# Hash attention with an MLP on one core: how queries without a matching key get their value, by a product or by an addition

## The chip, the cores and the metric

One NeuronCore of a Trainium2 chip runs the program. Five engines work in order, each on its own queue, and wait for each other by semaphores: TensorE (PE, matmul; its weight loads are listed as PEld), VectorE (DVE), ScalarE (ACT), GpSimd (POOL) and SyncE (SP, which only issues DMAs). PE writes its results into PSUM, from where DVE and ACT bring them to SBUF. The metric is the device time of one execution in microseconds (us).

## The reference

Queries, keys and values are `[4, 8, 768, 64]` (batch, head, token, width). Six random projections give each query and key a bucket of 6 bits; a query sees only keys of its own bucket.

```python
q_bits = einsum('bhsd,dk->bhsk', q, proj) > 0          # k the same
mask = q_bucket[:, :, :, None] == k_bucket[:, :, None, :]
scores = where(mask, scale * q @ k.T, -1e9)
attn = softmax(scores)                                  # per row
x = (attn @ v), heads side by side                      # [4, 768, 512]
xn = (x - mean) / sqrt(var + 1e-6) * g
out = x + relu(xn @ w1) @ w2                            # 512 -> 2048 -> 512
```

A row without any key of its bucket has only scores of -1e9. After the maximum is taken away they are all equal, so such a query gets the mean of all 768 values of its head. Both kernels compute this without a branch: every key gets an extra weight of `EPS_KEY = 2**-100` in every row. Beside a key that matches this is nothing; where none matches it is all there is, and the quotient is the mean.

## The kernel before

The bits are written as rows 64 to 69 under the transposed queries and keys (`slots`), scaled so that a score with different bits becomes hugely negative; one matmul of 70 rows then gives score and mask at once. The work is cut into 12 chunks of 256 queries (`b`, `t`: batch, third of the tokens). A chunk has four pairs of heads `j`, and each pair three units: PE forms four score tiles (L383, tile `sc`), ACT takes the exponential (L389, `ex`), and PE multiplies by the values (L415), eight products into the PSUM tile `av`. `vaug` holds the values in bf16 with a 65th column of ones, so the sum of weights comes out in column 64. After the third unit DVE takes the reciprocal of that column (L425) and multiplies (L426) into `x`.

The extra weight comes in at the first unit of a pair, by an opener (L406): a product of the constant matrix `epsk` (all `EPS_KEY`) with the values, broadcast over both query tiles. It carries `start=True`, all later products add to it. Its right side is either `vsum`, the sum of the six value blocks of a head, which POOL forms with five additions for half of the heads (`value_sums`, L336 and L339, 128x256 each), or, where that sum is not there in time, the six blocks of `vaug` themselves, in six products. The latter is so in five pairs of batch 0; all other 43 pairs have one opener.

The first 24 units, those of the chunks 0 and 1 with the score tiles of the next unit always formed one step ahead, are written out by hand (`first_two`): a list `seq` gives the units in order, and `also` names what goes between them: transposes of heads (`head`), hash products (`hash_pair`), loads and preparations for the next batch. From then on `interleave` lays each chunk's units out and puts fillers between them by their declared costs: the norm of the chunk before, its eight `up` blocks (L488, hidden layer; tile `hp`, evacuated to `hbuf` in turn by DVE at L129 and ACT at L133), the eight `down` parts of the chunk before that (L505, tile `o`; DVE adds them to `x` at L510, then SP stores), and the parts of `plan` that prepare the next batch: L and W load, N narrows to bf16 (POOL, L239), B and K transpose blocks (DVE, L244), T builds operands by DMA, H hashes, V casts values and sums them (POOL, L330 and L336 to L339), Q takes sums of squares (ACT, L191) for a safety test at the end. The norm gives `xn` (DVE, L450 to L452), `xnT` by a transposing DMA, and `rs` on POOL (L466, L467). After the last chunk come its norm, the downs left over, its ups and its downs. The order of instructions on an engine is that of these lists, but a scheduler may move neighbours.

PSUM: the score tiles have two buffers of two banks, `av` has two, and a third pool, `ps_mm`, has two that all other products share in turn (`hp`, `o`, hash, transposes). A tile of `ps_mm` can start only when DVE or ACT has emptied the buffer that it is given.

In batch 0 `CMAP` changes the order of the key blocks, and heads are transposed by PE instead of by DMA.

Of the kernel before, what the change touches and what calls it, by code (L numbers as in the profile page):

```python
# [9 lines left out]
F32 = mybir.dt.float32  # L10
BF16 = mybir.dt.bfloat16
# [17 lines left out]
def kernel(  # L29
# [11 lines left out]
    nc = tc.nc  # L41
# [57 lines left out]
    ]  # L99
    vsum = [  # L100
        consts.tile([P, H, D1], BF16, name=f"vsum{i}", tag=f"vsum{i}") for i in range(2)
    ]
    for i in range(2):
        nc.gpsimd.memset(vaug[i][:, :, :, D:D1], 1.0)
        nc.gpsimd.memset(vsum[i][:, :, D:D1], float(NC))

# [66 lines left out]
    class Prep:  # L173
# [13 lines left out]
        def squares(self, half, a, j):  # L187

            junk = work.tile([P, 2 * NC * D], BF16, tag="junk", bufs=1, name="junk")
            col = (2 * self.b + half) * 2 + j  # L190
            nc.scalar.activation(  # L191
                junk,
                self.tiles[half]["qk"[a]][:, 2 * j : 2 * j + 2].rearrange("p h c d -> p (h c d)"),
                AF.Square,
                accum_out=sq[:, a, col : col + 1],
            )
# [135 lines left out]
        def value_sums(self, half):  # L332
            hs = slice(half * H // 2, (half + 1) * H // 2)
            vn = self.va[:, hs, :, 0:D]
            acc = work.tile([P, H // 2, D], F32, tag="vacc", bufs=1, name="vacc")
            nc.gpsimd.tensor_add(acc, vn[:, :, 0, :], vn[:, :, 1, :])  # L336
            for c in range(2, NC):
                dst = self.vs[:, hs, 0:D] if c == NC - 1 else acc
                nc.gpsimd.tensor_add(dst, acc, vn[:, :, c, :])  # L339

        def part(self, kind, half):
# [7 lines left out]
            if kind in "BK":  # L349
                return [  # L350
                    (0, lambda a=a, j=j: self.blocks(half, a, j))
                    for a in range(kind == "K", 2) for j in range(2)
                ]
            if kind == "L":
                return [(0, lambda: self.load(half))]
# [9 lines left out]
    def att_units(b, t, x):  # L365
# [4 lines left out]
        for j in range(NP):  # L370
# [7 lines left out]
            for g, grp in enumerate(groups):  # L378
# [17 lines left out]
                def values(grp=grp, g=g, state=state, j=j, ha=ha):  # L396
                    if g == 0:
                        av = ps_av.tile([P, 2, TT, D1], F32, tag="av", name="av")
                        state["av"] = av
                        opens = (  # L400
                            [va[:, ha : ha + 2, c, :] for c in range(NC)]
                            if b == 0 and (t, j) in ((0, 0), (0, 2), (0, 3), (1, 2), (1, 3))
                            else [vs[:, ha : ha + 2, :]]
                        )
                        for i, o in enumerate(opens):
                            nc.tensor.matmul(  # L406
                                av,
                                epsk,
                                o.unsqueeze(2).to_broadcast([P, 2, TT, D1]),
                                start=(i == 0), stop=False, skip_group_check=True,  # L410
                            )
                    av = state["av"]
                    for i, (h, kj) in enumerate(grp):
                        for qi in range(TT):
# [3 lines left out]
                                va[:, h, CMAP[b][kj], :],  # L418
                                start=False,
                                stop=(g == 2 and i == 3),  # L420
                                skip_group_check=True,
                            )
                    if g == 2:
                        rc = work.tile([P, 2, TT], F32, tag="rc", name="rc")
                        nc.vector.reciprocal(rc, av[:, :, :, D])  # L425
                        nc.vector.tensor_tensor(  # L426
                            x[:, :, ha * D : (ha + 2) * D].rearrange(
                                "p t (h d) -> p h t d", h=2
                            ),
                            av[:, :, :, 0:D],  # L430
                            rc.unsqueeze(3).to_broadcast([P, 2, TT, D]),
                            op=AOP.mult,
                        )
# [179 lines left out]
    def first_two():  # L613
# [8 lines left out]
        def keep_awake(n):  # L622
            tp = ps_mm.tile([P, P], F32, tag="mm", name="wakep")
            for _ in range(n):
# [11 lines left out]
        load_w1()  # L636
        prep.value_sums(0)
        groups = [(0, 0), (0, 1), (1, 0), (1, 1), (2, 0), (3, 0), (2, 1), (3, 1)]
# [3 lines left out]
            0: [lambda: head(2), lambda: prep.values(1)],  # L642
            1: [lambda: head(3), lambda: nxt.load(0)],
            3: [lambda: prep.hash_pair(1, 0)],
# [4 lines left out]
            8: [  # L649
                lambda: prep.hash_pair(2, 1), lambda: nxt.load(1), lambda: nxt.load_v(0),  # L650
            ],
# [7 lines left out]
            15: [  # L659
                lambda: nxt.blocks(0, 0, 1), lambda: prep.value_sums(1),  # L660
            ],
# [16 lines left out]
    plan = {  # L678
        2: "K10 H10 N11 B11 V10 W11 | T11 H11 Q00 L20 V11 W20",
        3: "N20 B20 Q01 | T20 H20 L21",  # L680
        4: "V20 W21 Q10 L30 B21 N21 | T21 H21",
        5: "V21 W30 Q11 L31",
        6: "V30 W31 N30 B30 Q20 | T30 H30",
        7: "V31 Q21 B31 N31 | T31 H31",
        8: "Q30 Q31",
# [20 lines left out]
    for n in range(2, len(chunks)):  # L706
# [5 lines left out]
        fillers += mixed(early, tail[:4]) + ([(600, xtrans)] if n == 2 else [])  # L712
        fillers += mixed(late, tail[4:]) + ups
        tail = downs
        if n == NT * (B - 1):
# [197 lines left out]
```

## Time and profile before

| | |
|---|---|
| median of three runs | 327.76 us (326.68 to 327.8) |
| the profiled execution | 326.76 us, span of the profile 324.9 us |
| PE, busy | 306.4 us, 94% |
| weight loads (PEld) | 226.1 us, 70% |
| ACT | 217.3 us, 67% |
| DVE | 163.0 us, 50% |
| POOL | 90.5 us, 28% |
| granted TensorE clock, mean | 0.994 |

The page gives for each engine its busy time, then the span in 40 slices of 8.1 us, where each digit is the busy share in tenths. A group of instructions is one line: source line, engine, operation, output<-inputs, shapes, count; then busy time in us and mean duration of one in ns; then the idle time of the engine just before them and what ended it. Since matmuls overlap, the mean duration of one is longer than the distance from one to the next. The timeline lists instructions in order of time as start, length, engine, line, operation; a row can merge several. The chain of waits goes back from the last instruction to what released it, step by step.

### The profile page before, as it was taken

Reading aid. Unit: us, or ns where it says so; the run is one execution under the profiler, and the core shown is the slowest. Engines: PE = TensorE matmul, PEld = TensorE weight load, DVE = VectorE, ACT = ScalarE, POOL = GpSimd, SP = SyncE. Lnnn points to the kernel's source line nnn. Section 1 sums busy time; section 2 is a strip of 40 time slices with the busy share of each in tenths; the row PEclk is TensorE's granted clock in tenths of the full one; section 3 lists DMA queues with packets and bytes.
Section 4 is the critical chain, followed back from the end, with each engine's and each line's share of the span. In section 5 each row is a group of like instructions: output and inputs, shape, how many; then the busy total and the mean of one; then the engine's idle time right before and its main releaser. Section 6 shows DMA issues by size and latency. Waiting matters only on the chain.

```text
span 324.9 us, 7860 instructions
## 1 busy us (share of the span) xinstructions
PE 306.4 (94%) x3314; PEld 226.1 (70%) x3314; DVE 163.0 (50%) x321; ACT 217.3 (67%) x272; POOL 90.5 (28%) x117
## 2 busy tenths in 40 slices
PE   7958989999989999989999999999999999999992
PEld 5635568768758768759769769658679678687650
DVE  2668967653744654514654753532533623435320
ACT  5647689745766867876966966998657577574110
POOL 4777664662114060236090030200200100201100
PEclk9999999999999999999999999999999999999997
DMA  7999995986197398497255362020120210200301
GB/s 251 357 209 300 209 328 113 227 231 188 33 235 193 103 247 163 112 281 197 48 115 91 61 122 48 12 61 29 32 67 2 48 52 2 65 34 2 98 7 69
DMA packets 64874, 40.94 MB, mean 126 GB/s; under 512 B 47184, under 2 KB 59728, under 8 KB 64832
## 3 DMA queue, kind: packets, MB, share of 16 engines
q1 hardware_dynamic: 60368, 31.85, 39.2%
q0 software_dynamic: 4096, 8.13, 10.6%
q8 instruction: 28, 0.46, 0.6%
q10 hardware_dynamic: 368, 0.39, 0.4%
q14 instruction: 14, 0.11, 0.1%
HBM read 27.98 MB, written 6.88 MB: 107 GB/s over the span
## 4 chain that ended last, share of the span: by engine, by line
PE 73%; DMA 7%; ACT 6%; POOL 5%; DVE 4%; issue 4%; SPq 0%; ACTq 0%; POOLq 0%
PE hp L488 23%; PE o L505 20%; PE sc L383 14%; PE av L415 9%; DMA slots<-nat 4%; ACT junk L191 3%; ACT ex L389 2%; PE hash L275 2%; PE hash L306 2%; DVE slots L326 2%; DMA vnat<-in_v_dram 2%; POOL vaug L330 1%; PE av L406 1%; DMA qnat<-in_q_dram 1%; POOL vacc L339 1%
## 5 line engine op out<-in xcount | busy, mean ns | idle before, releaser
L389 ACT ACTIVATE ex<-sc,expb 128x1024 bf16<-128x1024 f32 x144 | 159.5, 1113 | 67.1 <-PE sc L383 66.9
L488 PE MATMUL hp<-xnT,w_sb 128*128 128x256 bf16 x768 | 98.6, 272 | 0.4 <-ACT hbuf L133 0.3
L505 PE MATMUL o<-w_sb,hbuf 128*128 128x512 bf16 x384 | 96.2, 379 | 0.0
L383 PE MATMUL sc<-slots 70*128 70x256 bf16 x576 | 87.3, 272 | 2.3 <-DVE slots L326 2.1
L488 PEld LDWEIGHTS <-w_sb 128*128 128x128 bf16 x768 | 72.0, 97 | 9.6 <-issue 0.8
L415 PEld LDWEIGHTS <-ex 128*128 128x128 bf16 x1152 | 53.1, 98 | 24.1 <-ACT ex L389 9.2
L415 PE MATMUL av<-vaug,ex 128*128 128x65 bf16 x1152 | 59.3, 194 | 3.8 <-ACT ex L389 3.7
L383 PEld LDWEIGHTS <-slots 70*128 70x128 bf16 x576 | 51.1, 97 | 16.9 <-DVE slots L326 2.6
L129 DVE TENSOR_SCALAR hbuf<-hp 128x512 bf16<-128x512 f32 x45 | 31.1, 691 | 58.4 <-PE hp L488 58.4
L505 PEld LDWEIGHTS <-hbuf 128*128 128x128 bf16 x384 | 35.2, 97 | 27.8
L466 POOL TENSOR_SCALAR rs<-mv 128x2 f32<-128x2 f32 x12 | 5.3, 442 | 168.0 <-DVE mv L451 168.0
L133 ACT ACTIVATE hbuf<-hp 128x512 bf16<-128x512 f32 x51 | 30.4, 596 | 20.9 <-PE hp L488 20.3
L510 DVE SCALAR_TENSOR_TENSOR x<-o,rs,x 128x512 f32<-128x512 f32 x24 | 17.8, 742 | 45.9 <-PE o L505 45.5
L426 DVE TENSOR_TENSOR x<-av,rc 128x256 f32<-128x256 f32 x48 | 20.3, 424 | 1.6
L452 DVE SCALAR_TENSOR_TENSOR xn<-x,mv,gbc 128x512 bf16<-128x512 f32 x24 | 19.5, 834 | 0.4 <-DVE mv L451 0.2
L425 DVE RECIPROCAL rc<-av 128x4 f32<-128x4 f32 x48 | 8.4, 176 | 18.2 <-PE av L415 18.2
L339 POOL TENSOR_TENSOR vacc<-vacc,vaug 128x256 f32<-128x256 f32 x24 | 16.9, 702 | 1.3
L450 DVE BATCH_NORM_STATS2 stats<-x 128x6 f32<-128x512 f32 x24 | 15.3, 677 | 0.2
L330 POOL CAST vaug<-vnat 128x1536 bf16<-128x1536 f32 x8 | 12.5, 1563 | 8.0 <-PE av L415 5.5
L239 POOL CAST nat<-qnat 128x1536 bf16<-128x1536 f32 x6 | 8.8, 1470 | 18.7 <-DMA qnat<-in_q_dram 13.3
L406 PE MATMUL av<-vsum,epsk 128*128 128x260 bf16 x43 | 11.9, 277 | 2.0 <-POOL vsum L339 2.0
L191 ACT ACTIVATE junk<-knat 128x768 bf16<-128x768 f32 x16 | 13.4, 840 | 0.2
(70 smaller groups left out, 195.0 us busy)
## 6 DMA issues: line engine op xcount, KB each, us to landing
out_dram<-x SPq DMA_DIRECT2D x24, 256.0 KB
vnat<-in_v_dram SPq DMA_DIRECT2D x7, 768.0 KB
qnat<-in_q_dram SPq DMA_DIRECT2D x11, 384.0 KB
knat<-in_k_dram SPq DMA_DIRECT2D x11, 384.0 KB
w_sb<-in_moe_w_ch_dram POOLq DMA_DIRECT2D x4, 1024.0 KB, 12.8
slots<-slots SPq DMA_DIRECT2D x6, 384.0 KB
qnat<-in_q_dram POOLq DMA_DIRECT2D x2, 768.0 KB, 11.9
knat<-in_k_dram POOLq DMA_DIRECT2D x2, 768.0 KB, 13.4
```

The costliest lines, as they stand in the source:

```text
L129: nc.vector.tensor_scalar_max(dst, src, 0.0)
L133: nc.scalar.activation(dst, src, AF.Relu if relu else AF.Copy)
L191: nc.scalar.activation(junk, self.tiles[half]["qk"[a]][:, 2 * j : 2 * j + 2].rearrange("p h c d -> p (h c d)"), AF.Square, accum_out=sq[:, ...
L339: nc.gpsimd.tensor_add(dst, acc, vn[:, :, c, :])
L383: nc.tensor.matmul(sc[:, i, :], sl[0:K1, h, 1, kj * P : (kj + 1) * P], sl[0:K1, h, 0, q0 : q0 + CT],)
L389: nc.scalar.activation(ex, sc, AF.Exp, bias=expb[:, 1:2] if b else expb[:, 0:1], scale=scale if b else scale / Q_SCALE,)
L415: nc.tensor.matmul(av[:, h - ha, qi, :], state[g][:, i, qi * P : (qi + 1) * P], va[:, h, CMAP[b][kj], :], start=False, stop=(g == 2 and i ...
L426: nc.vector.tensor_tensor(x[:, :, ha * D : (ha + 2) * D].rearrange("p t (h d) -> p h t d", h=2), av[:, :, :, 0:D], rc.unsqueeze(3).to_broa ...
L452: nc.vector.scalar_tensor_tensor(xn[:, :, i, :], x[:, i, :].rearrange("p (o d) -> p o d", d=P), mv[:, i, 0:1], gbc.rearrange("p (o d) -> p ...
L488: nc.tensor.matmul(hp[:, i, :], w1_sb[:, dt, nt * P : (nt + 1) * P], st["xnT"][:, dt, :], start=(dt == 0), stop=(dt == ND - 1),)
L505: nc.tensor.matmul(o2, st["h"][:, nt, i * P : (i + 1) * P], w2_sb[:, nt, :], start=(nt == 0), stop=(nt == NH - 1),)
L510: nc.vector.scalar_tensor_tensor(x[:, i, :], o2, st["rs"][:, i : i + 1], x[:, i, :], op0=AOP.mult, op1=AOP.add,)
```

## The change

From batch 1 on there are no openers. The first product of a pair starts the accumulation itself. The extra weight's share of the result is formed once for half of the heads of a batch: POOL sums the six blocks as before, the last addition giving the bf16 tile `vs16`; one product with `epsk` (`share`, part E of the plan) adds over the partitions; DVE copies the result to `vsum`, now in f32 and without a ones column. At the end of each pair DVE adds the constant `S * EPS_KEY` to the sums of weights, adds `vsum` to the products while it moves them to `x`, takes the reciprocal, and multiplies `x` in place: four instructions instead of two.

In batch 0 the first pair keeps its six products. For the others, PE sums the six blocks by products with the identity (`row_sums`, a tile of `ps_mm` for half of the heads), ACT copies the sums to `vrows`, and each pair has one opener with `vrows`. POOL forms no value sums in batch 0.

ACT's squares write over their own input (f32) instead of a spare bf16 tile. In the last chunk two of the eight `up` blocks of chunk 10 are held back until after its last unit.

```diff
-    vsum = [consts.tile([P, H, D1], BF16, ...) for i in range(2)]
+    vrows = consts.tile([P, H, D1], BF16)
+    vsum = [consts.tile([P, H, D], F32, ...) for i in range(2)]
...
-            junk = work.tile([P, 2 * NC * D], BF16, tag="junk", bufs=1, name="junk")
+            src = self.tiles[half]["qk"[a]][:, 2 * j : 2 * j + 2].rearrange("p h c d -> p (h c d)")
...
-                junk,
-                self.tiles[half]["qk"[a]][:, 2 * j : 2 * j + 2].rearrange("p h c d -> p (h c d)"),
+                src,
+                src,
...
+            acc = self.vs[:, hs]
+            self.vs16 = work.tile([P, H // 2, D], BF16, tag="vs16", bufs=1, name="vs16")
             nc.gpsimd.tensor_add(acc, vn[:, :, 0, :], vn[:, :, 1, :])
             for c in range(2, NC):
+                nc.gpsimd.tensor_add(self.vs16 if c == NC - 1 else acc, acc, vn[:, :, c, :])
+
+        def share(self, half):
+            ps = ps_mm.tile([P, H // 2 * D], F32, tag="mm", name="share")
+            nc.tensor.matmul(ps, epsk, self.vs16.rearrange("p h d -> p (h d)"))
+            nc.vector.tensor_copy(
+                self.vs[:, half * H // 2 : (half + 1) * H // 2].rearrange("p h d -> p (h d)"), ps
+            )
+
+        def row_sums(self, half):
+            hs = slice(half * H // 2, (half + 1) * H // 2)
+            ps = ps_mm.tile([P, H // 2, D1], F32, tag="mm", name="rows")
+            for c in range(NC):
+                nc.tensor.matmul(
+                    ps, ident, self.va[:, hs, c, :], start=(c == 0), stop=(c == NC - 1)
+                )
+            nc.scalar.activation(vrows[:, hs], ps, AF.Copy)
...
+            if kind == "E":
+                return [(110, lambda: self.share(half))]
...
-                        opens = (
-                            [va[:, ha : ha + 2, c, :] for c in range(NC)]
-                            if b == 0 and (t, j) in ((0, 0), (0, 2), (0, 3), (1, 2), (1, 3))
-                            else [vs[:, ha : ha + 2, :]]
-                        )
+                        opens = []
+                        if b == 0:
+                            opens = (
+                                [va[:, ha : ha + 2, c, :] for c in range(NC)]
+                                if (t, j) == (0, 0)
+                                else [vrows[:, ha : ha + 2, :]]
+                            )
...
-                                start=False,
+                                start=(b > 0 and (g, i, qi) == (0, 0, 0)),
...
+                        num = av[:, :, :, 0:D]
+                        if b == 0:
+                            nc.vector.reciprocal(rc, av[:, :, :, D])
+                        else:
+                            nc.vector.tensor_scalar_add(rc, av[:, :, :, D], S * EPS_KEY)
+                            nc.vector.tensor_tensor(
+                                xv, num,
+                                vs[:, ha : ha + 2, :].unsqueeze(2).to_broadcast([P, 2, TT, D]),
+                                op=AOP.add,
+                            )
+                            nc.vector.reciprocal(rc, rc)
+                            num = xv
                         nc.vector.tensor_tensor(
+                            xv, num, rc.unsqueeze(3).to_broadcast([P, 2, TT, D]), op=AOP.mult
                         )
...
-        prep.value_sums(0)
...
-            1: [lambda: head(3), lambda: nxt.load(0)],
+            1: [lambda: prep.row_sums(0), lambda: head(3), lambda: nxt.load(0)],
...
-                lambda: prep.hash_pair(2, 1), lambda: nxt.load(1), lambda: nxt.load_v(0),
+                lambda: prep.row_sums(1), lambda: prep.hash_pair(2, 1), lambda: nxt.load(1), lambda: nxt.load_v(0),
...
-                lambda: nxt.blocks(0, 0, 1), lambda: prep.value_sums(1),
+                lambda: nxt.blocks(0, 0, 1),
...
+        2: "K10 H10 N11 B11 V10 W11 | T11 H11 E10 Q00 L20 V11 W20",
+        3: "E11 N20 B20 Q01 | T20 H20 L21",
+        4: "V20 W21 Q10 L30 B21 N21 | T21 H21 E20",
+        5: "V21 W30 Q11 L31 | E21",
+        6: "V30 W31 N30 B30 Q20 | T30 H30 E30",
+        7: "V31 Q21 B31 N31 | T31 H31 E31",
...
-        fillers += mixed(late, tail[4:]) + ups
-        tail = downs
+        held = ups[-2:] if n == len(chunks) - 1 else []
+        fillers += mixed(late, tail[4:]) + ups[: len(ups) - len(held)]
+        tail = held + downs
```

## The prediction

> **What bounds the kernel now.** I read the page first: busy shares, then slices, then groups.
>
> ```profile
> PE 306.4 (94%) x3314; PEld 226.1 (70%) x3314; DVE 163.0 (50%) x321; ACT 217.3 (67%) x272; POOL 90.5 (28%) x117
> PE   7958989999989999989999999999999999999992
> L406 PE MATMUL av<-vsum,epsk 128*128 128x260 bf16 x43 | 11.9, 277 | 2.0 <-POOL vsum L339 2.0
> L426 DVE TENSOR_TENSOR x<-av,rc 128x256 f32<-128x256 f32 x48 | 20.3, 424 | 1.6
> L425 DVE RECIPROCAL rc<-av 128x4 f32<-128x4 f32 x48 | 8.4, 176 | 18.2 <-PE av L415 18.2
> ```
>
> PE is nearly full from slice 6 on; every other engine has room on average. A matmul's 277 ns is a latency, because matmuls overlap. What an opener (L406) costs is the step between starts, read in the timeline of a steady stretch:
>
> ```profile
> 229.84 1.03 PE L505 MATMUL o<-w_sb,hbuf 128*128 128x512 bf16 x4
> 230.70 0.28 PE L406 MATMUL av<-vsum,epsk 128*128 128x260 bf16 x1
> 230.81 0.41 PE L415 MATMUL av<-vaug,ex 128*128 128x65 bf16 x8
> 231.06 1.02 PE L505 MATMUL o<-w_sb,hbuf 128*128 128x512 bf16 x4
> ```
>
> The opener starts at 230.70 and the next product at 230.81: 0.11 us, with no gap on either side. In the same way eight av products take 0.25, four scores 0.44, a block of eight hp 0.87, four o 0.86. The steady part is bound by this row of starts.
>
> The first 62 us are otherwise. The chain of waits passes there through DVE, POOL and ACT; once PE stands for POOL:
>
> ```profile
> 18.11 0.66 POOL vsum L339
> 18.82 0.27 PE av L406
> 19.09 0.24 PE av L415 x8
> ```
>
> and in the timeline of ACT from 40 to 50 us the exponentials follow each other almost without a gap:
>
> ```profile
> 40.08 1.11 ACT L389 ACTIVATE ex<-sc,expb 128x1024 bf16<-128x1024 f32 x1 [0.30 <-PE sc L383]
> 41.44 3.24 ACT L389 ACTIVATE ex<-sc,expb 128x1024 bf16<-128x1024 f32 x3 [0.25 <-PE sc L383]
> 45.26 3.23 ACT L389 ACTIVATE ex<-sc,expb 128x1024 bf16<-128x1024 f32 x3 [0.57 <-PE sc L383]
> 48.74 2.25 ACT L389 ACTIVATE ex<-sc,expb 128x1024 bf16<-128x1024 f32 x2 [0.25 <-PE sc L383]
> ```
>
> There ACT is the bound, and its gaps (1.37 us together) are PE arriving late with the next scores, behind six openers of 0.68 us.
>
> **The change, part by part** (times on the clock of the profiled execution: span 324.9, run 326.76 us; the median of the three runs is 327.76, so the profiled one lies 1.0 below it).
>
> (a) Start, 12 to 37 us. The value sums of batch 0 leave POOL, and with them PE's 1.98 us wait at 16.8. In their place PE runs six products (6 x 0.11 = 0.67), ACT copies 128x260, and the rows tile takes a turn in the two ps_mm buffers. The copy is bounded by L221, 489 ns for 384 columns, and by its share by width, 0.33; I take 0.37. The queues give back most of the gain. The copy stands behind the exponential that ends at 15.08, so it ends at about 15.45; the k transposes of head 3 need that buffer and start there instead of at 14.10. Their ACT copy then ends at 16.5 instead of 15.47, the DVE casts L230/L231 behind it at 17.95, and the second hash product runs at 18.8 instead of 19.7. The scores that wait for its bits start at 21.05 instead of 21.90: -0.85. The second rows group stands in front of the hash product at 27.98, which the chain names: 0.67 less a gap of 0.03, +0.64. Sum -0.2; ends -1.98 (nothing given back) and +0.65 (only the second group counts).
>
> (b) 36 to 50 us. Four units lose five openers each, 20 x 0.11 = 2.2 us of PE. ACT bounds here, so what counts is its gaps: 1.37 go, less the 0.11 that remains before each: I take -1.25. Ends -2.2 and 0. From 50 to 62 ACT is busy throughout, which shifts the gain and does not consume it.
>
> (c) Batches 1 to 3: 36 openers x 0.111 = -4.0. Where the chain runs through ACT (85 to 91, 133 to 140, 205 to 217.6) some four of them are hidden, 0.45: -3.55. Ends -4.0 and -1.0.
>
> (d) Six share products (E): 6 x 0.11 = +0.66. Each waits for POOL's sum. The sums end at 62.8, 70.4, 117.7, 140.7, 165.5 and 189.7; the shares' places in the new instruction order correspond to 71.4, 84.8, 122.8, 143.5, 170.7 and 193.6, so no wait, the closest by 2.8. The single vs16 buffer makes V11's last POOL add wait from 69.7 for the share at 71.4; POOL's next work is at 87.8, so that costs nothing. Each share takes a ps_mm buffer. E11 leaves the next o tile the buffer of the hp tile just before it, which ACT evacuates from 84.55 to 85.15 while o would start at 84.90: +0.3. E20, E30 and E31 leave the next hp tile the share's buffer; DVE's copy (nearest row L426, 0.42) ends about 0.1 after PE is there: +0.3 in all, up to 1.1 each if that tile gets the o buffer instead. Taken +1.26; ends +0.66 and +4.3.
>
> (e) DVE. Each of 36 units gets a scalar add on 128x4 (nearest row the reciprocal, 0.176) and a 128x256 add (L426, 0.424): 36 x 0.6 = 21.6, and six copies 2.5; DVE goes to 187 of 325 us. The end of a unit holds DVE 1.2 us instead of 0.6. What is behind it is an hp evacuation (0.69, L129). A ps_mm buffer is wanted again 1.55 us after its hp block ends, and evacuation takes 0.17 + 0.69 + 0.04, so 0.65 is free. The worst order, av products followed directly by hp, delays the evacuation by 0.36. So 0, covered by that slack; uncovered it is the rival below. The av buffer is released after two instructions as before, and is wanted a unit (5.9 us) later. xnT comes 0.6 later and has some 4 us, except at the very end, (f). ScalarE's in-place squares (0.84, L191) write f32: ACT's f32 and bf16 rows (L221, L389) lie on one line of about 0.98 ns a column, so 0; they come after the readers of the same tile in the plan, and the load that waits for them waited before. Ends 0 and +5.5.
>
> (f) The end. In the timeline:
>
> ```profile
> 296.01 1.04 PE L488 MATMUL hp<-xnT,w_sb 128*128 128x256 bf16 x8
> 296.89 0.41 PE L415 MATMUL av<-vaug,ex 128*128 128x65 bf16 x8
> 297.09 0.60 ACT L133 ACTIVATE hbuf<-hp 128x512 bf16<-128x512 f32 x1 [0.82 <-PE hp L488]
> 297.13 7.07 PE L505 MATMUL o<-w_sb,hbuf 128*128 128x512 bf16 x32
> 304.06 7.44 PE L488 MATMUL hp<-xnT,w_sb 128*128 128x256 bf16 x64
> ```
>
> The 6.9 us of o products just cover the norm and its transpose. DVE's longer ending, with one hp evacuation put into the middle of the norm, makes xnT about 1.5 later; the two held hp blocks add 1.75 of cover. But now the o tile comes directly behind an hp block whose buffer it takes (in the build it waits for ACT): 0.17 + 0.04 + 0.60 + 0.04 = +0.85. That stall also adds cover, so none is left for xnT. Ends 0 and +1.5.
>
> Sum: -0.2 - 1.25 - 3.55 + 1.26 + 0 + 0.85 = -2.9; 326.76 - 2.9 = 323.9. A median of several runs lies somewhat above a low one; I say 324.3.
>
> **A rule of the Trainium skill.** By its own rows the DVE cast L452, with two SBUF inputs, takes 0.71 alone and 1.92 and 1.74 us while POOL casts at 54.7 and 56.1. The Trainium skill, "SBUF — State Buffer", section "Who interferes with whom", says that a VectorE instruction with two SBUF inputs and a GpSimd one that reads SBUF exclude each other for a whole instruction; these rows agree. The new multiplication reads x and rc, both in SBUF, where the old one read av from PSUM; by the rule (e) would be no longer 0, and the sum that of the third rival.
>
> **The rivals.**
> First, the start's gain is kept whole (-1.98): 323.9 - 1.8 = 322.1. For it: PE stood idle. Against: the ACT copy's place in its queue.
> Second, the openers' time turns into waits: as they filled PE while ACT worked, (b) gives 0 and (c) only -1.0, so 326.76 - 0.2 - 1.0 + 1.26 + 0.85 = 327.7. For it: PE's busy share is modelled. Against: no gap around 230.70. The Trainium skill, "Perfetto Trace Analysis", section "Identifying the Most-Contended Engine", judges TensorE's headroom by the weight loads' share, here 70%, not by matmul busy share; by it the spare would be 30% and this rival the case; the step of 0.11 contradicts that in the steady part.
> Third, slower: POOL and DVE exclude each other at the units' ends. From 85 to 190 POOL works some 35 of 105 us, so about 6 of 18 units collide, each up to 1.2 us; with the 0.36 above and less the slack of 0.65 an hp tile waits 0.9: 6 x 0.9 = +5.5, 329.4. It decides when three such collisions stand before an evacuation. Against: most units end with scores between them and the next evacuation.
> That the change does not remove the products is excluded by the built order: 17 openers and 18 sums remain of 73.
>
> **How the numbers follow.** Forecast 0.55 (322.8 to 326.0), first rival 0.12, second 0.18, third 0.15. The measurement can tell about 0.5% here: under 326.1 is faster, over 329.4 slower. Faster: the forecast's 0.55 less 0.05 for its upper tail, the first rival's 0.12, and 0.04 of the second, 0.66. Slower: 0.10 of the third rival, whose price lies at the bound and is open upwards, and 0.02 for the far ends of (d) and (f), 0.12. The rest, 0.22, is the same. The range goes from just under the first rival to just over the second, 321.8 to 327.9, and leaves out the third.
>
> **What would show it.** Right: L406 x17 with no wait on POOL; scores of heads 2 and 3 near 21 us; ACT from 40 to 50 without gaps; PE starts in step behind each unit; DVE near 187; one ACT wait of 0.6 to 0.9 after the last av. Wrong: PE waiting for DVE after hp blocks, L452 or the new multiplication stretched over 1 us beyond 85 us, idle PE before av where the opener stood, or share products waiting for POOL.

## The result and the profile after

| | before | after |
|---|---|---|
| median of 20 runs | 327.79 us (326.02 to 329.53) | 325.99 us (322.93 to 328.31) |
| ratio | | 0.9922 [0.9893, 0.9952] |
| profiled execution | 326.76 us, span 324.9 | 327.04 us, span 325.2 |
| its mean granted clock | 0.994 | 0.980 |

The change is faster by 0.8%, the way that was forecast, and the time lies in the range. By the medians it is 1.8 us where the forecast said 3.5 (from 327.76 to 324.3), and the forecast of 324.3 hits neither of the two heaps that after's runs form. Eight runs have a mean granted TensorE clock of 0.994 to 0.996 and take 322.9 to 324.0 us, mean 323.4. The other twelve have 0.973 to 0.980 and take 325.2 to 328.3, mean 326.7. The profiled execution is one of the twelve. The page after, busy shares, slices and granted clock:

```profile
PE 305.4 (94%) x3249; PEld 225.9 (69%) x3276; DVE 181.4 (56%) x399; ACT 216.8 (67%) x274; POOL 83.8 (26%) x105
PE   6888899999999999999999999989999999999991
PEclk9999967999999999999999999999999999999998
L462 DVE TENSOR_TENSOR x<-x,rc 128x256 f32<-128x256 f32 x36 | 20.7, 574 | 1.0
```

TensorE's busy time is nearly that of before and DVE has risen by 18 us, as the change says. The news is in the clock row: slices 6 and 7 read 6 and 7 where before had 9 throughout. The busy time by stretches, with the granted clock as the third column from the right; first before, then after:

```profile
38.00:40.00 2.00, 1.39 (x17) 0.90 (x16) 1.94 (x3) 1.79 (x2) 2.00 (x2) 1.00 1.24 208
40.00:42.00 2.00, 2.00 (x30) 1.50 (x28) 1.94 (x4) 1.67 (x2) 1.92 (x3) 1.00 1.16 339
46.00:50.00 4.00, 3.48 (x52) 3.05 (x53) 2.19 (x6) 3.73 (x5) 1.50 (x2) 1.00 1.32 239
```

```profile
38.00:40.00 2.00, 1.00 (x13) 0.70 (x14) 1.94 (x3) 1.55 (x2) 1.94 (x3) 1.00 1.25 209
40.00:42.00 2.00, 1.53 (x26) 1.17 (x25) 1.97 (x4) 1.69 (x2) 1.11 (x1) 1.00 1.20 289
46.00:50.00 4.00, 4.00 (x36) 3.00 (x34) 1.65 (x5) 2.98 (x4) 1.50 (x2) 0.50 1.32 219
```

The first number behind the length is PE's busy time. From 38 to 42 us PE was busy 3.39 of 4 us before and 2.53 after; this is the stretch from which the change took openers. From 42.5 to 52.8 us the clock then stands at one half. In 46 to 50 PE is busy all the time, and yet ACT, the bound there, gets only 2.98 us of work instead of 3.73.

At the start and at the end the predicted rows are there. PE's timeline after (in brackets the idle time before, and who ended it):

```profile
14.35 0.85 PE L354 MATMUL rows<-vaug,ident 128*128 128x260 bf16 x6
15.04 0.49 PE L211 MATMUL tpose<-identf,qnat 128*128 128x128 f32 x3
15.99 0.55 PE L211 MATMUL tpose<-identf,knat 128*128 128x128 f32 x3 [0.46 <-ACT vrows L357]
...
18.62 0.29 PE L428 MATMUL av<-vrows,epsk 128*128 128x260 bf16 x1
...
21.44 0.50 PE L403 MATMUL sc<-slots 70*128 70x256 bf16 x3 [0.72 <-DVE slots L326]
...
294.06 0.41 PE L437 MATMUL av<-vaug,ex 128*128 128x65 bf16 x8
294.31 1.91 PE L519 MATMUL hp<-xnT,w_sb 128*128 128x256 bf16 x16
296.90 7.07 PE L536 MATMUL o<-w_sb,hbuf 128*128 128x512 bf16 x31 [0.69 <-ACT hbuf L133]
```

The wait for POOL is gone, the k transposes of head 3 wait for the copy of the row sums, and the last o tile waits 0.69 us for ACT.

### The profile page after: what moved, and what is told of

Same layout as the page of the kernel before. It is cut to its first block, busy times and chain, and to the rows that moved or that the text cites. A ratio compares the mean times of both kernels' runs of the same rounds, so it can differ in the third digit from the quotient of the medians.

```text
span 325.2 us, 7843 instructions
## 1 busy us (share of the span) xinstructions
PE 305.4 (94%) x3249; PEld 225.9 (69%) x3276; DVE 181.4 (56%) x399; ACT 216.8 (67%) x274; POOL 83.8 (26%) x105
## 3 DMA queue, kind: packets, MB, share of 16 engines
q1 hardware_dynamic: 60368, 31.85, 39.2%
## 4 chain that ended last, share of the span: by engine, by line
PE 81%; ACT 9%; DVE 5%; issue 3%; ACTq 0%; DVEq 0%
PE hp L519 25%; PE o L536 21%; PE sc L403 17%; PE av L437 10%; ACT ex L409 4%; PE hash L275 3%; DVE slots L326 2%; PE hash L306 2%; ACT qnat L191 1%; ACT knat L191 1%; PE tpose L211 1%; PE wakep L656 1%; DVE bits L311 1%; ACT hbuf L133 1%; DVE slots L231 1%
## 5 line engine op out<-in xcount | busy, mean ns | idle before, releaser
L536 PE MATMUL o<-w_sb,hbuf 128*128 128x512 bf16 x357 | 92.4, 379 | 1.9 <-ACT hbuf L133 0.7
L403 PE MATMUL sc<-slots 70*128 70x256 bf16 x576 | 90.0, 278 | 3.3 <-DVE slots L326 2.9
L437 PEld LDWEIGHTS <-ex 128*128 128x128 bf16 x1152 | 54.4, 99 | 22.6 <-ACT ex L409 9.3
L437 PE MATMUL av<-vaug,ex 128*128 128x65 bf16 x1152 | 60.8, 196 | 2.6 <-ACT ex L409 2.4
L462 DVE TENSOR_TENSOR x<-x,rc 128x256 f32<-128x256 f32 x36 | 20.7, 574 | 1.0
L454 DVE TENSOR_SCALAR rc<-av 128x4 f32<-128x4 f32 x36 | 5.7, 158 | 23.6 <-PE av L437 23.6
L483 DVE SCALAR_TENSOR_TENSOR xn<-x,mv,gbc 128x512 bf16<-128x512 f32 x24 | 18.0, 766 | 0.1
L330 POOL CAST vaug<-vnat 128x1536 bf16<-128x1536 f32 x8 | 12.2, 1525 | 10.5 <-DMA vnat<-in_v_dram 5.5
L455 DVE TENSOR_TENSOR x<-av,vsum 128x256 f32<-128x256 f32 x36 | 14.9, 413 | 0.0
L191 ACT ACTIVATE knat<-knat 128x768 f32<-128x768 f32 x16 | 13.5, 848 | 0.0
L191 ACT ACTIVATE qnat<-qnat 128x768 f32<-128x768 f32 x16 | 13.5, 844 | 0.0
## 6 DMA issues: line engine op xcount, KB each, us to landing
knat<-in_k_dram POOLq DMA_DIRECT2D x2, 768.0 KB, 14.6
```

The lines of the kernel that those rows point to most:

```text
L191: nc.scalar.activation(src, src, AF.Square, accum_out=sq[:, a, col : col + 1],)
L403: nc.tensor.matmul(sc[:, i, :], sl[0:K1, h, 1, kj * P : (kj + 1) * P], sl[0:K1, h, 0, q0 : q0 + CT],)
L437: nc.tensor.matmul(av[:, h - ha, qi, :], state[g][:, i, qi * P : (qi + 1) * P], va[:, h, CMAP[b][kj], :], start=(b > 0 and (g, i, qi) == ( ...
L462: nc.vector.tensor_tensor(xv, num, rc.unsqueeze(3).to_broadcast([P, 2, TT, D]), op=AOP.mult)
L483: nc.vector.scalar_tensor_tensor(xn[:, :, i, :], x[:, i, :].rearrange("p (o d) -> p o d", d=P), mv[:, i, 0:1], gbc.rearrange("p (o d) -> p ...
L536: nc.tensor.matmul(o2, st["h"][:, nt, i * P : (i + 1) * P], w2_sb[:, nt, :], start=(nt == 0), stop=(nt == NH - 1),)
```

## The experiments

The question is what makes the low clock, and what each part is worth without it. "Whole clock" below means runs at a mean of 0.993 or more; it isn't 1, because in every profile the clock also falls to a half in the last microseconds, behind the last product. Before itself is no steady measure: of the 71 runs of it taken beside the experiments, 25 are at whole clock (mean 326.30), 6 at 0.989 to 0.990 (327.4), 23 at 0.985 to 0.986 (328.1) and 17 at 0.980 to 0.982 (329.5). The prediction's sum started from an execution of the first kind.

**The twenty openers put back (after, four pairs of batch 0).**

```diff
-                                if (t, j) == (0, 0)
+                                if (t, j) in ((0, 0), (0, 2), (0, 3), (1, 2), (1, 3))
```

> The changed kernel with the six products in place of one vrows opener again in the four pairs (0,2), (0,3), (1,2), (1,3) of batch 0: 20 products of 0.11 us come back between 36 and 50 us. Theory A: TensorE's clock falls to a half from 42.5 to 52.8 us in 12 of 20 runs of the changed kernel because TensorE has too little to do between 36 and 42 us once these 20 products are gone. Then no run here is below a mean granted clock of 0.99, and the time is 323.4 (the changed kernel's runs at 0.994 to 0.996) plus 0 to 1.25: 323.4 to 324.7. Theory B: the half-clock stretch has nothing to do with these products (a matter of chance or of the chip, or of the smaller load in batches 1 to 3). Then again about half of the runs are at 0.973 to 0.980 and the median is 326 to 327.5.

Measured: 324.15 us, ratio 0.9904 [0.9871, 0.9937]; nine runs between 0.989 and 0.997, none near 0.98; one, at 0.989, is just under the 0.99 that theory A gave as the least. The heap near 0.98 is gone with more work for PE. Theory A holds.

**Products that do nothing, in the same place (after).**

```diff
+                    if b == 0 and t < 2 and j > 1:
+                        for _ in range(3):
+                            nc.tensor.matmul(
+                                av, wake,
+                                vrows[:, ha : ha + 2, :].unsqueeze(2).to_broadcast([P, 2, TT, D1]),
+                                start=False, stop=False, skip_group_check=True,
+                            )
```

> The changed kernel with three extra products of a zero weight matrix into av ahead of each group of av products of the pairs (0,2), (0,3), (1,2), (1,3) of batch 0 (36 products, 0.33 us per unit, adding nothing to the result), where TensorE otherwise waits for an exponential. Theory A: the clock stays whole in all runs; as the products lie in waits, the time is that of the changed kernel's undisturbed runs, 323.4, up to 324.0. Theory B: half of the runs keep a half-clock stretch, median 326 to 327.

Measured: 323.58 us, ratio 0.9875 [0.9833, 0.9918]; six runs, all at 0.993 or more. The busy row of the stretch shows the difference from after:

```profile
38.00:40.00 2.00, 1.64 (x25) 1.32 (x22) 1.93 (x4) 1.50 (x2) 2.00 (x2) 1.00 1.24 220
40.00:42.00 2.00, 2.00 (x32) 1.61 (x30) 1.14 (x3) 1.98 (x3) 0.00 (x0) 1.00 1.09 389
46.00:50.00 4.00, 4.00 (x60) 3.61 (x58) 1.23 (x4) 3.62 (x5) 0.75 (x2) 1.00 1.26 182
```

36 products more, and the kernel is 2.4 us faster by the medians. Their content is nothing; what they change is that PE is busy.

**The batch-0 part alone (before, with row sums and vrows).**

```diff
+        def row_sums(self, half):          # as in the change
...
-                            if b == 0 and (t, j) in ((0, 0), (0, 2), (0, 3), (1, 2), (1, 3))
-                            else [vs[:, ha : ha + 2, :]]
+                            if b == 0 and (t, j) == (0, 0)
+                            else [(vs if b else vrows)[:, ha : ha + 2, :]]
...
-        prep.value_sums(0)
...
-                lambda: nxt.blocks(0, 0, 1), lambda: prep.value_sums(1),
+                lambda: nxt.blocks(0, 0, 1),
```

> The kernel before with the batch-0 part of the change alone: row sums by TensorE, copied by ScalarE, one vrows opener in eleven of the twelve pairs, no POOL sums in batch 0; batches 1 to 3 keep their openers, and nothing of the end is changed. By the prediction's terms (a) and (b) 326.76 - 0.2 - 1.25 = 325.3 at whole clock. Theory A: half or more of the runs have the half-clock stretch after 42 us all the same, and stand 3.2 higher, near 328.5. Theory B in the form that the smaller load of batches 1 to 3 lowers the clock: all runs at 0.994, near 325.3.

Measured: 328.47 us, ratio 1.0015 [0.9987, 1.0044]; twelve runs, all at 0.977 to 0.982. The batch-0 part alone brings the low clock, and with it no gain at all. Here the profile shows it from 39.2 to 52.8 us, again behind a thin stretch:

```profile
38.00:39.00 1.00, 0.30 (x4) 0.12 (x3) 0.97 (x2) 0.85 (x1) 1.00 (x2) 1.00 1.26 206
39.00:40.00 1.00, 1.00 (x13) 0.86 (x12) 0.97 (x3) 0.64 (x1) 1.00 (x1) 0.57 1.24 222
40.00:44.00 4.00, 4.00 (x38) 2.77 (x37) 2.50 (x5) 2.77 (x4) 0.16 (x1) 0.50 1.07 380
```

**The same with the products that do nothing.** The edit is that of the second experiment, on top of the third.

> The kernel before with the batch-0 part alone and the three zero products ahead of each av group of the four pairs (0,2), (0,3), (1,2), (1,3). Theory A: all runs at 0.993 or more, where without the zero products all 12 stood at 0.977 to 0.982. The time then measures terms (a) and (b) without the clock: 326.3 - 1.45 = 324.9, 323.5 if the start's gain is kept whole, 326.1 if the openers' time turned into waits. Theory B: the low clock stays, 328.5.

Measured: 325.97 us, ratio 0.9943 [0.9914, 0.9972]; of twelve runs ten at whole clock, mean 325.9, two at 0.989 and 0.991, which theory A did not allow. The profile is of one of these two: its half clock stands from 12.9 to 16.3 us, far ahead of the products that do nothing, and the stretch from 36 to 53 us keeps its clock. So the products cure their own stretch and no other. Terms (a) and (b) together are worth 325.9 - 326.3 = -0.4 at whole clock, not -1.45.

**Batches 1 to 3 alone (after, with batch 0 as before).**

```diff
+    vsum0 = consts.tile([P, H, D1], BF16, ...)      # bf16, for batch 0
...
-                                if (t, j) == (0, 0)
-                                else [vrows[:, ha : ha + 2, :]]
+                                if (t, j) in ((0, 0), (0, 2), (0, 3), (1, 2), (1, 3))
+                                else [vsum0[:, ha : ha + 2, :]]
...
-            1: [lambda: prep.row_sums(0), lambda: head(3), lambda: nxt.load(0)],
+            1: [lambda: head(3), lambda: nxt.load(0)],
```

> The changed kernel with batch 0 as it was before: POOL's value sums, the six products in five pairs, vsum in bf16 for the others; the share and the DVE addition from batch 1 on, the squares in place and the two held up blocks stay. By terms (c), (d), (f) -3.55 + 1.26 + 0.85 = -1.44 against before at equal clock: 326.3 (mean of before's seven runs at 0.994 to 0.996) - 1.44 = 324.9 where the clock is whole. Theory A: batch 0 decides on the clock, so the runs have the clocks of before, a third of them whole and the others 1.6 or 3 us higher, median 326 to 328. Rival: the smaller load of batches 1 to 3 lowers the clock in other places, and no run is over 0.99.

Measured: 325.75 us, ratio 0.9906 [0.9865, 0.9947]; the clocks spread from 0.977 to 0.994. Three of twelve runs are at whole clock, mean 323.8, that is -2.5 against before and not -1.44. So this part gives more than forecast, and it keeps before's unsteady clock, as theory A says in its widened form. In its first form, on record before the low clocks of before itself had been noticed, it said that no run of this kernel would be below 0.99; seven of the twelve are.

**Before, once more with a profile.**

> The kernel before, once more with a profile. Of 20 of its runs 7 had a mean granted clock of 0.994 to 0.996 (326.0 to 326.7 us), the others 0.985 to 0.986 (327.8 to 327.9) or 0.981 to 0.982 (329.1 to 329.5). Theory A, widened: before has the same half-clock stretch in about two of three runs, where TensorE is lightly loaded in batch 0, and the profile of 326.76 us was one of the others; expected, if this run is one of those at 327.8 or more: PEclk at 0.50 for 5 to 9 us between 38 and 55 us. Rival: its slower runs have the low clock elsewhere, or spread thinly over the span.

Measured: 327.75 us at 0.985, the kind that is wanted. The slices' granted clock, and PE's timeline and the stretches (clock third from the right) around the drop:

```profile
PEclk9969999999999999999999999999999999999998
```

```profile
15.91 0.85 PE L306 MATMUL hash<-qkT,proj 128*32 128x384 f32 x8
18.51 0.27 PE L406 MATMUL av<-vsum,epsk 128*128 128x260 bf16 x1 [1.75 <-POOL vsum L339]
...
19.55 1.51 PE L306 MATMUL hash<-qkT,proj 128*32 128x384 f32 x8
```

```profile
18.00:19.00 1.00, 0.49 (x11) 0.46 (x11) 0.23 (x1) 0.00 (x0) 1.00 (x2) 1.00 1.14 208
19.00:20.00 1.00, 1.00 (x9) 0.37 (x10) 0.00 (x0) 0.29 (x1) 1.00 (x2) 0.58 1.17 217
20.00:24.00 4.00, 3.41 (x24) 1.73 (x17) 2.13 (x4) 1.32 (x2) 2.29 (x3) 0.50 1.08 210
```

The half clock comes at 19.2 us, not between 38 and 55 as I had expected of the widened theory: right behind the wait for POOL's value sum. The hash products take 1.51 us instead of 0.85. The stretch of 36 to 42 us, which still has the openers, keeps its clock.

**Before, with products that do nothing in that wait.**

```diff
+                        zeros = 16 if (b, t, j) == (0, 1, 0) else 0
+                        for z in range(zeros):
+                            nc.tensor.matmul(
+                                av, wake,
+                                va[:, ha : ha + 2, 0, :].unsqueeze(2).to_broadcast([P, 2, TT, D1]),
+                                start=(z == 0), stop=False, skip_group_check=True,
+                            )
```

> The kernel before with 16 zero products of 0.11 us (1.8 us) into av where TensorE waits 1.98 us for POOL's value sum at 16.8 us. The trace of a run of before at clock 0.985 has its half-clock stretch from 19.2 to 26.0 us, right behind this wait. Theory A: that stretch goes, the runs that stood at 0.981 to 0.986 join the others: nearly all at 0.993 or more, 326.0 to 326.8. Rival: the wait is not what lowers the clock, and half or more of the runs stay at 0.986 or less, 327.7 to 330.

Measured: 326.32 us, ratio 0.9969 [0.9946, 0.9992]; twelve runs at 0.992 to 0.998, where the kernel before had 11 of 17 at 0.990 or less beside it. The products take the place of the wait:

```profile
16.64 2.01 PE L407 MATMUL av<-vaug,wake 128*128 128x260 bf16 x16
18.60 0.27 PE L414 MATMUL av<-vsum,epsk 128*128 128x260 bf16 x1
18.71 0.40 PE L423 MATMUL av<-vaug,ex 128*128 128x65 bf16 x8
```

So the kernel before had a low clock of its own in about two runs of three, from POOL's wait. The change took this wait away and made a new thin stretch 20 us later.

**The end: one held block, and none (after with the products that do nothing).**

```diff
-        held = ups[-2:] if n == len(chunks) - 1 else []
+        held = ups[-1:] if n == len(chunks) - 1 else []
```

> The changed kernel with the zero products in batch 0 (which stood at 323.58 us) and only one up block held back instead of two. With two, the o tile behind the last av products takes the buffer of the second held block and waits 0.69 us for ScalarE. With one, the o tile takes the buffer of a block emptied long before, and starts at once; xnT then has 6.9 + 0.87 us of cover where 6.9 + 1.75 + 0.69 were used to 6.9 + 1.75 without a wait. If xnT is in time: -0.7, 322.9. If xnT comes too late (predicted 1.5 later than before, for which 6.9 us were just enough): the wait moves behind the o products, 0 to -0.3 only.

> The same with no up block held back. The longer ending on DVE makes xnT some 1.5 us later than before, where 6.9 us of o products just covered it: PE waits for xnT 0.5 to 1.5 us behind the o products, and the o tile ahead waits for nothing: between -0.2 and +0.8 against 323.58. If holding back two blocks was needless: -0.7.

Measured: 323.30 (322.24 to 325.28) and 323.60 us (323.15 to 324.00), beside 323.58 with two held blocks: the runs spread too far to tell these three apart. The traces do. From the first exponential to the start of DVE's last addition they take 302.65 us with one held block and 303.04 with none, where two take 303.46. The timeline shows why, first with one, then with none:

```profile
292.56 1.04 PE L527 MATMUL hp<-xnT,w_sb 128*128 128x256 bf16 x8
293.44 7.07 PE L544 MATMUL o<-w_sb,hbuf 128*128 128x512 bf16 x31
300.34 7.43 PE L527 MATMUL hp<-xnT,w_sb 128*128 128x256 bf16 x64
```

```profile
292.84 0.41 PE L445 MATMUL av<-vaug,ex 128*128 128x65 bf16 x8
293.09 7.07 PE L544 MATMUL o<-w_sb,hbuf 128*128 128x512 bf16 x31
300.41 7.44 PE L527 MATMUL hp<-xnT,w_sb 128*128 128x256 bf16 x64 [0.25 <-DMA xnT<-xn]
```

With two held blocks PE waits 0.68 ahead of o, with one for nothing, with none 0.25 behind o for xnT. The second held block is what costs: with one, the expected -0.7 is there (-0.8). With none it is -0.4, between the two cases that were expected: xnT was late, but by less than 0.5 to 1.5 us.

**DVE's addition done twice.** The addition into `x` (L455) is issued a second time with the same values.

> The changed kernel with the zero products, and the DVE addition of vsum at the end of each pair of batches 1 to 3 done twice (the second writes the same values): 36 more DVE instructions of 0.42 us, 15 us of DVE in all. Term (e) says that DVE's longer endings lie in the slack of the buffers: 0 to +0.5 in all. The third rival (the new endings reach the evacuations) would give +0.4 at each of some 10 to 36 endings, +4 to +15.

Measured: 322.96 us (322.65 to 323.10). The medians would make it faster than the kernel without the second addition; that lies at the two ends (see below on the last stretch). A measure without the ends is the time from the first exponential of chunk 3 to the first of chunk 11, the 37th and the 133rd of all. Up to these two, PE has the same number of score, av and hp products behind it in all kernels here, and the time repeats: 188.36 to 188.38 us in the seven profiles of the changed kernel and of those variants that leave its batches 1 to 3 as they are, 191.45 to 191.48 in the five of before and its variants. With the zero products:

```profile
81.26 1.11 ACT L409 ACTIVATE ex<-sc,expb 128x1024 bf16<-128x1024 f32 x1
...
269.62 1.11 ACT L409 ACTIVATE ex<-sc,expb 128x1024 bf16<-128x1024 f32 x1 [0.45 <-PE sc L403]
```

and with the addition doubled as well:

```profile
81.47 1.11 ACT L409 ACTIVATE ex<-sc,expb 128x1024 bf16<-128x1024 f32 x1
...
269.92 1.11 ACT L409 ACTIVATE ex<-sc,expb 128x1024 bf16<-128x1024 f32 x1 [0.45 <-PE sc L403]
```

188.36 and 188.46 us: 32 of the 36 second additions, some 13 us of DVE, cost 0.1. DVE's longer endings are covered, and not by little.

**Without the shares.** The six E entries are taken out of `plan`.

> The changed kernel with the zero products and without the six share products and their DVE copies: the part that brings in the mean for queries without a key is left out of batches 1 to 3, vsum then holds unfinished sums. Term (d): six products of 0.11 and 0.6 of stalls at their buffers, -1.26 against 323.58: 322.3. If the shares stall nothing: -0.66.

Measured: 322.72 us (322.24 to 322.97), 0.9 below the kernel with shares by the medians. In the two profiles, 0.5 of the difference lies behind the last addition (7.47 and 6.94 us from there to the end). The same two exponentials, without shares:

```profile
81.26 1.11 ACT L409 ACTIVATE ex<-sc,expb 128x1024 bf16<-128x1024 f32 x1
...
269.19 1.11 ACT L409 ACTIVATE ex<-sc,expb 128x1024 bf16<-128x1024 f32 x1 [0.45 <-PE sc L403]
```

188.36 with and 187.93 without: five of the six shares lie in this stretch and cost 0.43 together, which is less than their five products of 0.11. PE's first wait for an exponential behind E11, with shares and without, tells why:

```profile
89.14 0.42 PE L445 MATMUL av<-vaug,ex 128*128 128x65 bf16 x8 [0.31 <-ACT ex L409]
```

```profile
89.14 0.42 PE L445 MATMUL av<-vaug,ex 128*128 128x65 bf16 x8 [0.72 <-ACT ex L409]
```

The products start at the same time; without the shares PE only waits 0.41 longer for the exponential. What E11 takes is time in which PE would have waited for ACT. The other four shares cost their products, 4 x 0.11.

**The second group of row sums later.**

```diff
-                lambda: prep.row_sums(1), lambda: prep.hash_pair(2, 1), lambda: nxt.load(1), ...
+                lambda: prep.hash_pair(2, 1), lambda: nxt.load(1), ...
...
-            11: [lambda: prep.hash_pair(3, 0)],
+            11: [lambda: prep.hash_pair(3, 0), lambda: prep.row_sums(1)],
```

> The version with the zero products and one held block, and the second group of row sums moved from ahead of the hash product of heads 4 and 5 (27.4 us) to behind the first hash product of heads 6 and 7 (34.8 us). Term (a) put the second group's place at +0.64, by the hash product behind it, which was on the chain. If it is so, and hash and scores of heads 6 and 7 come earlier with it: -0.3 to -0.6 against 323.1 (that version at whole clock). Rival: the scores of heads 6 and 7, which wait for their bits, give it back in the new place: 0, and if vrows comes too late for the pair at 36.4 us, up to +0.5.

Measured: 322.79 us, ratio to before 0.9873 [0.9832, 0.9915], against 323.30 without the move; whole-clock means 322.8 and 323.1, with spreads of 0.5 and 0.8, so not told apart. In the trace the scores behind the group come 0.7 us earlier by the third exponential as origin (14.6 instead of 15.3 for the 11th), and four exponentials later all of it is given back (23.1 in both). The rival holds.

The versions with the zero products, with one held block (323.30, ratio 0.9877 [0.9832, 0.9922]) or with the row sums later as well (322.79), stand below both kernels: 1.2 to 1.3% under before, where the change alone has 0.8%.

## Why the prediction was right, and where it was wrong

**The sum.** At whole clock before has a mean of 326.30 (25 runs) and after 323.41 (8 runs): -2.9, and the sum was -2.9. That it agrees so well is luck. The traces of before and of after with the zero products, both at whole clock, split the time:

| stretch | predicted | measured |
|---|---|---|
| start of the span to the first exponential | 0 | 10.93 - 11.48 = -0.55 |
| from there to the first exponential of chunk 3: (a), (b), one share | -0.2 - 1.25 + 0.11 = -1.34 | 70.33 - 71.14 = -0.8 |
| from there to the first of chunk 11: 32 openers, five shares | -3.1 + 1.15 = -1.95 | 188.36 - 191.48 = -3.1 |
| from there to the last addition: four openers, (f) | -0.44 + 0.85 = +0.41 | 44.77 - 44.41 = +0.36 |
| last addition to the end of the span | 0 | 7.47 - 6.39 = +1.1 |

Before's two exponentials are these:

```profile
82.62 1.11 ACT L389 ACTIVATE ex<-sc,expb 128x1024 bf16<-128x1024 f32 x1
...
274.10 1.11 ACT L389 ACTIVATE ex<-sc,expb 128x1024 bf16<-128x1024 f32 x1 [0.45 <-PE sc L383]
```

From the first exponential to the last addition the work is 3.6 shorter, not 2.9. Too much was forecast for the start and too little for batches 1 to 3, and the two ends, for which nothing was forecast, bring the total back towards -2.9. (The first exponential comes between 10.6 and 12.2 us in the fourteen profiles.)

**(a)** was right in mechanism and size: the queue of ACT gave the start's gain back as described. The scores of heads 2 and 3 came at 21.44 in the profile (forecast 21.05, in a run whose first hash product started 1.15 us later); counted from the first exponential, the exponential behind these scores came 1.0 earlier (0.85 forecast), and the second rows group took 0.7 of it again (0.64 forecast); 0.3 is left, for a forecast of 0.2. The first rival, the whole gain kept, is out.

**(b)** is the step that failed in size. "1.37 go, less the 0.11 that remains before each: I take -1.25" took ACT's gaps for the work of the openers. (It also took away the 0.11 once, where it remains before each of four units; that reading gives -0.93.) With the openers put back at whole clock, the first exponential of chunk 3 is only 0.25 later than with the zero products (70.58 and 70.33 us behind the first exponential). The zero products stand in the openers' places, but they take little themselves: the whole-clock runs have a mean of 323.41 without them and 323.58 with them, and the spread is larger than that. Against before, all that the change and the zero products do between the 14th exponential and the first of chunk 3 is worth 0.5 (0.33 earlier at the one, 0.81 at the other). So most of the gaps had another cause than the openers; the one of 0.36 to 0.7 us in which the scores wait for DVE's bits is one that the trace names. Between 36 and 51 us ACT waits 3.0 us for scores before, 2.4 with the openers put back and 1.8 with the zero products, and part of the difference is lost again up to chunk 3. In batch 0 the second rival was right in the main: the openers had mostly filled time in which PE waited.

**(c)** was right in mechanism and somewhat too small: without shares the stretch from chunk 3 to chunk 11 is 191.48 - 187.93 = 3.55 shorter than before, and that is 32 openers at 0.111 in full. The 0.45 that was taken off as hidden behind ACT isn't seen; PE waits 1.9 us for exponentials between 84 and 290 us before and with the zero products alike. For these openers the second rival is out.

**(d)** was too dear. Of its +1.26 the trace bears out 0.43, the four products of batches 2 and 3. E20, E30 and E31, with 0.3 of stalls in all, show no wait in the trace. E11's 0.3 is there (in the profile after, the share starts at 87.28 and the o tile behind it at 87.69, 0.41 later where the step is 0.11), but the next wait for an exponential takes all of it up. E10 costs nothing either: with and without it the first exponential of chunk 3 starts at 81.26 in both profiles.

**(e)** was right: 0, and 0.1 for twice the addition. DVE's busy time rose by 18.4 us, not by the 24.1 that were forecast. The third rival's mechanism is in the profile, and about as often as it said, but not its price. The new multiplication took 574 ns on average and 424 in the median, since five of the 36 ran beside a POOL cast and took 1.04 to 1.70 us, one of the signs that the prediction gave for being wrong. In the timeline after:

```profile
119.86 1.47 POOL L330 CAST vaug<-vnat 128x1536 bf16<-128x1536 f32 x1
119.91 1.13 PEld L275 LDWEIGHTS hash<-bt,proj 128*32 128x32 f32 x32 [0.21 <-DVE x L455]
119.92 1.51 PE L275 MATMUL hash<-bt,proj 128*32 128x192 f32 x32
120.02 1.58 DVE L462 TENSOR_TENSOR x<-x,rc 128x256 f32<-128x256 f32 x1
```

The multiplication at 120.02 takes 1.58 us instead of 0.42, and PE goes on.

**(f)** was right as a mechanism: 0.69 of wait for 0.85 forecast, no wait for xnT behind two held blocks. That it also said that without held blocks xnT would be late is borne out by 0.25 us. Against before, the stretch with (f) and the last four openers is +0.36, for +0.41 forecast.

**What was missing** is the clock. The sum used an execution at 0.994 and the text asked of each removed product what time it takes, never what its being there does. That is the step that put the median wrong: 324.3 was forecast and 325.99 came. The median of after stands 2.6 above its whole-clock mean, that of before 1.5 above its own. The change removed one cause of a low clock and added another; this took 1.1 of the 2.9 us, and left 1.8 between the medians. Filling the new hole brings most of it back.

## What to carry to other kernels

A product that hides behind another engine's wait costs nothing and can still be worth something: before taking it away, look at how busy TensorE is left over the next few microseconds, and at the granted clock of more runs than the profiled one. Where runs of a kernel fall into heaps, sort them by granted clock first and compare like with like; a sum made from one execution belongs to that execution's heap. If a light stretch can't be filled with work, products of zeros in waits that are there anyway are a cheap cure for that wait (36 of them brought 2.4 us to the changed kernel by the medians, 16 brought 1.3 to the kernel before).

## What the runs showed of the hardware that I had not expected

**The clock falls without any long pause, and for whole periods.** In after no gap of PE between 39 and 42.5 us is longer than 0.7 us. Over the 3.41 us ahead of each drop PE's matmuls cover 0.49 (before), 0.61 (after), 0.70 (batch 0 alone), 0.59 and 0.60 (the two other profiles with a drop) of the time by the trace. The half clock then lasts 3.41, 3.41, 6.83, 10.24 and 13.65 us in these five profiles: one, one, two, three and four times 3.41. The Trainium skill, "TensorE: Matmul & The Clock Gate", section "Part 1: The HAM clock gate (the "warmup" mystery)", has a free-running window of 3413 ns that decides between half and full clock; these lengths agree with it. So do the stretches of whole clock between them: in after 37.55 us ahead of the drop and 269.65 behind it, 11 and 79 times 3.413. A free-running window would also explain why the same kernel is hit in some runs only. The same page's section "HAM oscillation — how this bites in real kernels" asks for no idle gap over about 3.4 us; here the longest gaps were 0.7 and 1.75 us and the clock fell, so looking at the longest gap alone is not enough. That the work of TensorE in such a stretch decides is shown by the experiments, which changed it both ways; what share of it is enough is not. The profile of before that kept its clock has a stretch of 3.41 us with a share of 0.42 (up to 18.9 us), and from 20.75 to 24.15 us it has PE busy 2.01 of 3.40 us; batches 1 to 3 alone have the same 2.01 of 3.40 from 21.3 to 24.7 us, and lose the clock there. The share before batch 0 alone lost it was higher, 0.70. Why all twelve runs of batch 0 alone were hit but only twelve of twenty of the whole change isn't settled either.

**The last stretch has two lengths.** From the last addition to the end of the span the five profiles of before and of its variants take 6.38 to 6.46 us, and so does the one with the doubled addition (6.44); the other eight of the changed kernel's family take 6.90 to 7.47. In the six short ones 4 packets on the queue that loads instructions fall into that stretch, in the eight long ones 5. That a fifth packet is the cause was not tried, but it goes with 0.5 to 1.1 us in all fourteen profiles, and it may be why the kernel with more work on DVE has the lower median: its profile has the short end, the one without the second addition the long one. Only the profiled execution of each kernel shows its end, so this stays open.
